# Writing a linear-attention read-out transposed, by 32-column tiles, so that the layer behind it needs no transposes

## Chip, cores, metric

One of the eight cores of a Trainium2 chip. The metric is the device time of one execution in microseconds (us), median of several, without the profiler's own span being used for it.

## The reference, cut to what matters

```python
def _attn_ref(q, k, v, alpha):                      # (4, 8, 768, 48) each
    for t in range(S):
        state = alpha[:, :, t, :, None] * state + einsum('bhd,bhe->bhde', k[:, :, t], v[:, :, t])
        y[:, :, t] = einsum('bhd,bhde->bhe', q[:, :, t], state)

def _moe_ref(x, w_in, w_out, g_ln):                 # x is y as (3072, 384); w_in (384, 1024)
    h = x @ w_in
    solu = h * softmax(h)
    ln = (solu - mean(solu)) / sqrt(var(solu) + 1e-06) * g_ln
    return ln @ w_out
```

The kernel works in 24 tiles of 128 tokens, four batches side by side, six tiles of each in turn. In a tile the recurrence becomes masked scores (128x128 a head), a read of the state carried from the tile before, and an update of the state. The first tile of each batch has no state to read. All matmuls are in fp32, and w_in and w_out arrive as 64-bit numbers and are converted on the chip.

## The kernel before: the parts that matter

```python
ps_tp = pool("ps_tp", 2, space=PS)     # transposes, two buffers for all of them
...
def scores(n):                          # per pair j of heads, the two heads in two row halves
    for j in range(NP):
        for i in range(2):
            nc.tensor.matmul(a[i][:, j], lhsT=d["kT"][heads[i], j], rhs=d["qT"][heads[i], j], ...)
...
def read_out(n):
    y = ps_o.tile([P, H, D], FP, tag="o", name="y")         # tokens on partitions
    if c:
        for j in range(NP):                                  # state: 4 matmuls, 96 columns moving
            nc.tensor.matmul(y[:, 2*j:2*j+2, :], lhsT=d["qT"][:, j], rhs=states[b][:, j]..., ...)
    for h in range(H):                                       # v: 8 matmuls, 48 columns moving
        nc.tensor.matmul(y[:, h, :], lhsT=d["sT"][:, h % 2, h // 2], rhs=d["v"][:, h], ...)
    nc.scalar.copy(out=d["x"], in_=y...)
...
def x_T(n):                                                  # x to features on partitions
    tp = ps_tp.tile([P, KC, P], FP, tag="tp", name="tp_x")
    for a in range(KC):                                      # KC = 3
        nc.tensor.transpose(out=tp[:, a], in_=d["x"][:, a*P:(a+1)*P], identity=ident)
    nc.scalar.copy(out=d["xT"], in_=tp)
...
# one turn of the loop, cut: loads; transposes of alpha, q (n+1); up projection (n-1), first half;
# scores (n); transposes of k (n+1); up projection, second half; keys_back, read_out, next_state (n);
# down projection (n-3); x_T (n).  A scheduler then orders each engine's instructions.
```

Of the kernel before, what the change touches and what calls it, by code (L numbers as in the profile page):

```python
# [9 lines left out]
FP = mybir.dt.float32  # L10
U8 = mybir.dt.uint8
U32 = mybir.dt.uint32
I32 = mybir.dt.int32
AF = mybir.ActivationFunctionType
ALU = mybir.AluOpType
AX = mybir.AxisListType
P = 128
# [15 lines left out]
def fast_path(ctx, tc, q, k, v, alpha, moe_w_in, moe_w_out, moe_g_ln, out):  # L33
# [9 lines left out]
    nc = tc.nc  # L43
    B, H, S, D = q.shape
    NTOK, DM = out.shape
# [3 lines left out]
    NP = H // 2  # L49
    DP = 64  # L50
    KC = DM // P
# [5 lines left out]
    def pool(name, bufs, **kw):  # L57
        return ctx.enter_context(tc.tile_pool(name=name, bufs=bufs, **kw))

    const = pool("const", 1)  # L60
    vp = pool("vp", 4)
    work = pool("work", 2)
    small = pool("small", 4)
    xtp = pool("xtp", UP + 2)
    hid = pool("hid", DOWN - UP + 1)
    rawp = pool("rawp", 4)
    wtmp = pool("wtmp", 2)
    ps_tp = pool("ps_tp", 2, space=PS)
    ps_a = pool("ps_a", 1, space=PS)
    ps_h = pool("ps_h", 2, space=PS)  # L70
    ps_o = pool("ps_o", 2, space=PS)

    ident = const.tile([P, P], FP, name="ident")
    mask = const.tile([P, P], FP, name="mask")
    ones = const.tile([P, P], FP, name="ones")
    w_in = const.tile([P, KC, DFF], FP, name="w_in")
    w_out = const.tile([P, FC, DM + 1], FP, name="w_out")
# [9 lines left out]
    NIN = 4  # L87
    qn = [const.tile([P, H, DP], FP, name=f"qn{i}") for i in range(NIN)]
    kn = [const.tile([P, H, DP], FP, name=f"kn{i}") for i in range(NIN)]
    an = [const.tile([P, H, DP], FP, name=f"an{i}") for i in range(NIN)]  # L90
    SW = P + 1
    aT = [const.tile([P, NP, SW], FP, name=f"aT{i}") for i in range(2)]
    seed = [const.tile([P, NP, SW], FP, name=f"seed{i}") for i in range(2)]
    hT = [const.tile([P, NP * SW + 1], FP, name=f"hT{i}") for i in range(2)]
    unit = const.tile([P, NP, SW], FP, name="unit")
    states = [const.tile([P, NP, 2, D], FP, name=f"state{b}") for b in range(B)]

    st = [dict() for _ in range(N)]
    halves = [slice(0, DP), slice(DP, 2 * DP)]
# [2 lines left out]
    def place(n):  # L102
        c, b = divmod(n, B)
        return b, c

    def load(n):
        b, c = place(n)
        st[n]["v"] = vp.tile([P, H, D], FP, name="vn")
        for src, dst in (
            (alpha, an[n % NIN][:, :, 0:D]),  # L110
            (q, qn[n % NIN][:, :, 0:D]),
            (k, kn[n % NIN][:, :, 0:D]),
            (v, st[n]["v"]),
        ):
            nc.sync.dma_start(out=dst, in_=src[b, :, c * P : (c + 1) * P, :].rearrange("h p d -> p h d"))

# [50 lines left out]
    def decayed(n):  # L167

        b, c = place(n)
        if c == 0:  # L170
            return
        h4 = hT[n % 2][:, 0 : NP * SW].rearrange("p (j s) -> p j s", s=SW)
        s = states[b].rearrange("p j i e -> p j (i e)")
        nc.gpsimd.tensor_tensor(  # L174
            out=s, in0=s, in1=h4[:, :, 1:2].to_broadcast([P, NP, 2 * D]), op=ALU.mult
        )

    def scores(n):
# [19 lines left out]
        nc.scalar.copy(out=d["kg"], in_=tp)  # L198

    def read_out(n):  # L200
        b, c = place(n)
        d = st[n]
        y = ps_o.tile([P, H, D], FP, tag="o", name="y")
        if c:
            for j in range(NP):
                nc.tensor.matmul(  # L206
                    y[:, 2 * j : 2 * j + 2, :], lhsT=d["qT"][:, j],
                    rhs=states[b][:, j].rearrange("p i e -> p (i e)"),
                    start=(j == 0), stop=False, skip_group_check=True,
                )  # L210
        for h in range(H):
            nc.tensor.matmul(  # L212
                y[:, h, :], lhsT=d["sT"][:, h % 2, h // 2], rhs=d["v"][:, h],
                start=(c == 0 and h == 0), stop=(h == H - 1), skip_group_check=True,
            )
        d["x"] = work.tile([P, DM], FP, name="x")
        nc.scalar.copy(out=d["x"], in_=y.rearrange("p h d -> p (h d)"))

    def next_state(n):
        b, c = place(n)  # L220
        d = st[n]
        if c == NCH - 1:
            return
        kv = ps_o.tile([P, NP, 2, D], FP, tag="o", name="kv")
        for j in range(NP):
            nc.tensor.matmul(  # L226
                kv[:, j].rearrange("p i e -> p (i e)"), lhsT=d["kg"][:, j],
                rhs=d["v"][:, 2 * j : 2 * j + 2, :], start=True, stop=True,
            )
        for i in range(2):  # L230
            r = halves[i]
            new = states[b][r, :, i]
            if c == 0:
                nc.vector.tensor_copy(out=new, in_=kv[r, :, i])
            else:
                nc.vector.tensor_tensor(out=new, in0=new, in1=kv[r, :, i], op=ALU.add)

    def x_T(n):
        d = st[n]
        tp = ps_tp.tile([P, KC, P], FP, tag="tp", name="tp_x")  # L240
        for a in range(KC):
            nc.tensor.transpose(out=tp[:, a], in_=d["x"][:, a * P : (a + 1) * P], identity=ident)  # L242
        d["xT"] = xtp.tile([P, KC, P], FP, name="xT")
        nc.scalar.copy(out=d["xT"], in_=tp)  # L244

    HF = FC // 2

# [72 lines left out]
    for i in range(NIN):  # L320
        nc.vector.memset(an[i], 1.0)
        nc.gpsimd.memset(qn[i], 0.0)
        nc.gpsimd.memset(kn[i], 0.0)
    load(0)
    nc.scalar.dma_start(
        out=mask, in_=nc.inline_tensor(np.triu(np.ones((P, P), np.float32)), name="mask_c").ap()
# [15 lines left out]
    float64 = moe_w_in.dtype != FP  # L342
    IN, OUT = 512, DM
    pieces = [(0, a, s) for s in range(0, DFF, IN) for a in range(KC)] + [(1, f, 0) for f in range(FC)]

    def words(i):
        kind, c, s = pieces[i]
        rows = slice(c * P, (c + 1) * P)
        src = moe_w_out[rows, :] if kind else moe_w_in[rows, s : s + IN]
        dst = w_out[:, c, 0:DM] if kind else w_in[:, c, s : s + IN]  # L350
        return src, dst

    def fetch(i):
        src, dst = words(i)
        if not float64:
            nc.sync.dma_start(out=dst, in_=src)
            return None
        raw = rawp.tile([P, dst.shape[1], 2], U32, tag="raw", name="raw")
        nc.sync.dma_start(out=raw.rearrange("p f w -> p (f w)"), in_=src.bitcast(U32))
        return raw  # L360

    raws = {}

    def convert(i):
        kind, c, _ = pieces[i]
        _, dst = words(i)
        if float64:
            raw = raws.pop(i)
            lo, hi = raw[:, :, 0], raw[:, :, 1]
            F = dst.shape[1]  # L370
            low = wtmp.tile([P, F], FP, tag="low", name="low")
            top = wtmp.tile([P, F], U32, tag="top", name="top")
            power = wtmp.tile([P, F], U32, tag="power", name="power")
            nc.scalar.activation(out=low, in_=lo, func=AF.Copy, scale=2.0**-52)
            nc.vector.tensor_scalar(
                out=top, in0=hi, scalar1=3, scalar2=0x3FFFFFF8, op0=ALU.logical_shift_left, op1=ALU.bitwise_and
            )
            nc.vector.scalar_tensor_tensor(  # L378
                out=top, in0=hi, scalar=0xC0000000, in1=top, op0=ALU.bitwise_and, op1=ALU.bitwise_or
            )  # L380
            nc.vector.tensor_scalar(out=power, in0=top, scalar1=0xFF800000, scalar2=None, op0=ALU.bitwise_and)
            nc.gpsimd.tensor_tensor(out=low, in0=low, in1=power.bitcast(FP), op=ALU.mult)  # L382
            eng = nc.vector if i % 2 else nc.gpsimd
            eng.tensor_tensor(out=dst, in0=low, in1=top.bitcast(FP), op=ALU.add)
        if kind:

            nc.scalar.mul(out=dst, in_=dst, mul=g_col[:, c : c + 1])
# [47 lines left out]
    for n in range(N + DOWN):  # L435
        if n + 2 < N:
            load(n + 2)
        if n < DOWN:
            mine = range(nout + n * FC // DOWN, nout + (n + 1) * FC // DOWN)
            for i in mine:  # L440
                raws[i] = fetch(i)
        m, l = n - UP, n - DOWN
        now, rise, fall, after = n < N, 0 <= m < N, l >= 0, n + 1 < N
        if after:
            prep_aq(n + 1)
        if l > 0:
            finish(l - 1)
        if now:
            decayed(n)
        if after:  # L450
            prep_scan(n + 1)
        if rise:
            up(m, 0)
        if after:
            prep_q(n + 1)
        if now:
            scores(n)
        if after:
            prep_k(n + 1)
        if n == 0:  # L460
            for i in range(KC, 2 * KC):
                convert(i)
        if rise:
            up(m, 1)
            partial(m)
        if n < DOWN:
            for i in mine:
                convert(i)
        if n == DOWN:
            centre()  # L470
        if now:
            keys_back(n)
            read_out(n)
            next_state(n)
        if fall:
            down(l)
        if now:
            x_T(n)
        if 2 * DOWN <= n < 2 * DOWN + len(pieces):
            in_range(n - 2 * DOWN)  # L480
    finish(N - 1)
# [472 lines left out]
```

## Time and profile before

| | |
|---|---|
| time, median | 490.15 us (489.24 to 491.8, 3 runs); 489.69 with the runs beside the changed kernel |
| busy, whole span | PE 461.1 us, DVE 264.8, POOL 196.1, ACT 172.7 |
| one tile in the middle | 18.43 us, PE full |
| first down projection done, start of its follower | 94.52 us |

PE is TensorE's matmuls, PEld its weight loads, POOL is GpSimd. Lengths of matmuls overlap, so a price is read from differences of starts. The lines themselves stand in the prediction, where each is used. The last row of the table splits the run into a start and the regular rest; this line of the timeline of the kernel before carries it (columns: start, length, engine, line of the kernel, what, count):

```profile
94.52 0.49 PE L242 MATMUL tp_x<-ident,x 128*128 128x128 f32 x3
```

### The profile page before, as it was taken

What the parts mean: (1) busy time and instruction counts of PE and PEld (TensorE: products, weight loads), DVE (VectorE), ACT (ScalarE), POOL (GpSimd) and SP (SyncE); (2) the same over time, 40 slices, a digit from 0 to 9 for tenths busy, and PEclk for the clock granted to TensorE, in tenths of its full rate; (3) what the DMA queues carried; (4) which work ended last, traced back from release to release, by engine and by line L of the source; (5) the groups of instructions that cost most, each with busy time, mean ns of one, the idle gap of its engine ahead of it and who ended that gap; (6) DMA issues with size and microseconds to landing.
All of it is one profiled execution on the core that took longest, in us unless ns stands there. A gap on an engine that the chain in (4) does not pass through costs nothing.

```text
span 490.0 us, 8081 instructions
## 1 busy us (share of the span) xinstructions
PE 461.1 (94%) x3195; PEld 389.1 (79%) x3195; DVE 264.8 (54%) x522; ACT 172.7 (35%) x344; POOL 196.1 (40%) x208
## 2 busy tenths in 40 slices
PE   2488989999999999999999999999999999999993
PEld 1377978798798798798798798798798798788761
DVE  5897798655365275275275275375374264353231
ACT  3143544588333333333232232232233243333210
POOL 6686476442342342342342342342352352352130
PEclk9998769999999999999999999999999999999998
DMA  8795464687133133133133133033031000000001
GB/s 243 182 230 128 114 130 93 169 254 212 30 68 66 29 69 66 25 71 66 23 71 69 22 70 73 19 71 74 19 70 29 16 17 17 17 1 17 17 16 40
DMA packets 107679, 36.92 MB, mean 75 GB/s; under 512 B 100713, under 2 KB 104049, under 8 KB 107633
## 3 DMA queue, kind: packets, MB, share of 16 engines
q1 hardware_dynamic: 107328, 36.19, 30.6%
q8 instruction: 27, 0.44, 0.4%
q14 instruction: 20, 0.16, 0.1%
q10 hardware_dynamic: 304, 0.14, 0.1%
HBM read 31.59 MB, written 4.72 MB: 74 GB/s over the span
## 4 chain that ended last, share of the span: by engine, by line
PE 87%; DVE 6%; POOL 3%; DMA 2%; issue 1%; ACT 0%; SPq 0%; POOLq 0%; DVEq 0%
PE o L290 26%; PE h L258 24%; PE y L212 8%; PE a L183 7%; PE tp L120 7%; PE kv L226 4%; PE y L206 4%; PE tp_k L196 2%; PE o L285 2%; POOL low L382 2%; PE tp_x L242 2%; DVE top L378 1%; DMA raw<-in_moe_w_in_dram 1%; DVE qF L144 1%; PE mean L415 1%
## 5 line engine op out<-in xcount | busy, mean ns | idle before, releaser
L258 PE MATMUL h<-xT,w_in 128*128 128x128 f32 x1152 | 138.4, 277 | 0.0
L258 PEld LDWEIGHTS h<-xT,w_in 128*128 128x128 f32 x1152 | 134.5, 194 | 0.5
L290 PE MATMUL o<-w_out,u 128*128 128x385 f32 x384 | 130.5, 491 | 0.0
L290 PEld LDWEIGHTS o<-w_out,u 128*128 128x128 f32 x384 | 70.9, 190 | 45.0
L311 POOL TENSOR_TENSOR r<-sums,mhalf 128x1 f32<-128x1 f32 x24 | 13.2, 551 | 141.7 <-DVE sums L307 141.7
L300 DVE COPY sums<-o 128x3 f32<-128x3 f32 x24 | 3.9, 160 | 98.9 <-PE o L290 98.9
L244 ACT COPY xT<-tp_x 128x384 f32<-128x384 f32 x24 | 11.5, 479 | 124.8 <-PE tp_x L242 124.8
L212 PE MATMUL y<-vn,sT 128*128 128x48 f32 x384 | 49.4, 283 | 2.4 <-DVE sT L188 2.4
L212 PEld LDWEIGHTS y<-vn,sT 128*128 128x128 f32 x384 | 48.2, 203 | 3.0 <-DVE sT L188 2.8
L183 PE MATMUL a<-qT,kT 48*128 48x128 f32 x384 | 44.3, 311 | 6.3 <-POOL qT L155 5.2
L264 DVE TENSOR_TENSOR u<-h,e 128x512 f32<-128x512 f32 x48 | 32.8, 684 | 31.4 <-ACT e L263 31.3
L134 DVE TENSOR_TENSOR_SCAN hT<-aT,unit 128x516 f32<-128x516 f32 x24 | 31.1, 1295 | 33.8 <-ACT aT L121 33.7
L265 ACT ACTIVATE u<-u 128x512 f32<-128x512 f32 x48 | 30.3, 630 | 51.9 <-DVE u L264 51.8
L183 PEld LDWEIGHTS a<-qT,kT 48*128 48x128 f32 x384 | 33.6, 200 | 14.3 <-POOL qT L155 5.3
L155 POOL TENSOR_TENSOR qT<-qT,qF 128x512 f32<-128x512 f32 x24 | 29.2, 1216 | 38.7 <-DVE qF L144 38.7
L263 ACT ACTIVATE e<-h 128x512 f32<-128x512 f32 x48 | 28.6, 595 | 44.5 <-PE h L258 44.5
L162 POOL TENSOR_TENSOR kT<-kT,hT 128x508 f32<-128x508 f32 x24 | 30.2, 1258 | 21.2 <-ACT kT L121 21.2
L273 POOL TENSOR_TENSOR part_e<-e 128x512 f32<-128x512 f32 x24 | 30.9, 1287 | 17.8 <-ACT e L263 17.8
L174 POOL TENSOR_TENSOR state<-state,hT 128x384 f32<-128x384 f32 x20 | 16.7, 835 | 46.0 <-DVE hT L134 46.0
L144 DVE TENSOR_TENSOR_SCAN qF<-aT,seed 128x516 f32<-128x516 f32 x24 | 32.3, 1344 | 0.7
L188 DVE TENSOR_TENSOR sT<-a,mask 128x512 f32<-128x512 f32 x48 | 31.0, 678 | 0.0
L273 DVE TENSOR_TENSOR part_u<-u 128x512 f32<-128x512 f32 x24 | 18.4, 765 | 15.6 <-ACT u L265 15.6
(87 smaller groups left out, 588.1 us busy)
## 6 DMA issues: line engine op xcount, KB each, us to landing
raw<-in_moe_w_in_dram SPq DMA_DIRECT2D x12, 512.0 KB, 6.1
raw<-in_moe_w_out_dram SPq DMA_DIRECT2D x16, 384.0 KB, 4.5
vn<-in_v_dram SPq DMA_DIRECT2D x24, 192.0 KB, 2.7
an<-in_alpha_dram SPq DMA_DIRECT2D x24, 192.0 KB, 3.3
qn<-in_q_dram SPq DMA_DIRECT2D x24, 192.0 KB, 3.6
kn<-in_k_dram SPq DMA_DIRECT2D x24, 192.0 KB, 2.8
out_dram<-o_sb SPq DMA_DIRECT2D x24, 192.0 KB, 2.0
ident<-ident_c ACTq DMA_DIRECT2D x1, 64.0 KB, 1.9
```

The costliest lines, as they stand in the source:

```text
L120: nc.tensor.transpose(out=tp[:, j], in_=src[:, 2 * j : 2 * j + 2, :], identity=ident)
L134: nc.vector.tensor_tensor_scan(out=h[:, 0 : NP * SW][:, ::-1], data0=a.rearrange("p j s -> p (j s)")[:, ::-1], data1=unit.rearrange("p j s ...
L144: nc.vector.tensor_tensor_scan(out=d["qF"].rearrange("p j s -> p (j s)"), data0=a.rearrange("p j s -> p (j s)"), data1=s.rearrange("p j s ...
L162: nc.gpsimd.tensor_tensor(out=d["kT"][:, :, 0 : P - 1], in0=d["kT"][:, :, 0 : P - 1], in1=hT[n % 2][:, 0 : NP * SW].rearrange("p (j s) -> ...
L183: nc.tensor.matmul(a[i][:, j], lhsT=d["kT"][heads[i], j], rhs=d["qT"][heads[i], j], start=True, stop=True)
L188: nc.vector.tensor_tensor(out=d["sT"][:, i], in0=a[i], in1=mask[:, None, :].to_broadcast([P, NP, P]), op=ALU.mult)
L212: nc.tensor.matmul(y[:, h, :], lhsT=d["sT"][:, h % 2, h // 2], rhs=d["v"][:, h], start=(c == 0 and h == 0), stop=(h == H - 1), skip_group_ ...
L258: nc.tensor.matmul(h[:, f], lhsT=w_in[:, a, (f0 + f) * P : (f0 + f + 1) * P], rhs=d["xT"][:, a], start=(a == 0), stop=(a == KC - 1),)
L264: nc.vector.tensor_tensor(out=d["u"][:, fs], in0=h, in1=d["e"][:, fs], op=ALU.mult)
L265: nc.scalar.activation(out=d["u2"][:, fs], in_=d["u"][:, fs], func=AF.Square)
L273: eng.tensor_tensor(out=t, in0=d[key][:, 0:HF], in1=d[key][:, HF:FC], op=ALU.add)
L290: nc.tensor.matmul(o[:, 0 : DM + 1], lhsT=d["u"][:, f], rhs=w_out[:, f], start=(f == 0), stop=(f == FC - 1), skip_group_check=True,)
```

## The change

The intent: use v and the state as the stationary operand, so that y comes out with features on partitions, as the up projection wants it. 48 features of a head don't fit a group of 32 partitions; so the first 32 of each head fill two blocks of 128 features, and the remaining 16 of two heads share a group in a third. The rows of w_in are loaded in the same order.

```diff
 def read_out(n):
-    y = ps_o.tile([P, H, D], FP, tag="o", name="y")
+    y = ps_o.tile([P, KC, P], FP, tag="o", name="y")
+    def mm(a, r, lhsT, rhs, stop=False):
+        nc.tensor.matmul(y[32*r:32*r+32, a], lhsT=lhsT, rhs=rhs, start=r not in begun, stop=stop,
+                         skip_group_check=True, tile_position=(0, 32*r))
     if c:
-        ... 4 matmuls, rhs = state
+        for a in range(2):
+            for r in range(NP):
+                h = NP*a + r
+                mm(a, r, states[b][:, h//2, h%2], d["qT"][:, h//2])
+        for r in range(NP):
+            mm(2, r, states[b][:, r, 2], d["qT"][:, r])
-    ... 8 matmuls, rhs = v
+    for a in range(2):
+        for r in range(NP):
+            h = NP*a + r
+            mm(a, r, vt[:, h, 0:E0], d["sT"][:, h%2, h//2])
+    for i in range(2):
+        for r in range(NP):
+            mm(2, r, vt[:, 2*r+i, last[i]], d["sT"][:, i, r], stop=i == 1)
-    nc.scalar.copy(out=d["x"], in_=y...)
+    nc.scalar.copy(out=d["xT"], in_=y)
-def x_T(n): ...
@@ loads
-    (v, st[n]["v"]),
+    (v[:, :, :, 0:E0], vt[:, :, 0:E0]), (v[:, :, :, E0:D], vt[:, :, 48:48+E1]),   # E0, E1 = 32, 16
@@ w_in, per piece of 128 rows and 512 columns
-    one transfer of 128 rows
+    4 transfers of 32 rows, or 8 of 16
@@ next_state: the state is updated in four pieces for two; four memsets of v's buffers at the start
```

More of the change, by code (lines that the diff above doesn't have):

```diff
@@ L60, in fast_path @@
     const = pool("const", 1)
-    vp = pool("vp", 4)
     work = pool("work", 2)
@@ L90, in fast_path @@
     an = [const.tile([P, H, DP], FP, name=f"an{i}") for i in range(NIN)]
+    E0, E1 = 32, 16
+    vn = [const.tile([P, H, 80], FP, name=f"vn{i}") for i in range(NIN)]
+    last = [slice(48, 80), slice(32, 64)]
     SW = P + 1
@@ L95, in fast_path @@
     unit = const.tile([P, NP, SW], FP, name="unit")
-    states = [const.tile([P, NP, 2, D], FP, name=f"state{b}") for b in range(B)]
+    states = [const.tile([P, NP, 3, E0], FP, name=f"state{b}") for b in range(B)]
     st = [dict() for _ in range(N)]
@@ L107, in load @@
         b, c = place(n)
-        st[n]["v"] = vp.tile([P, H, D], FP, name="vn")
+        vt = vn[n % NIN]
         for src, dst in (
@@ L112, in load @@
             (k, kn[n % NIN][:, :, 0:D]),
-            (v, st[n]["v"]),
+            (v[:, :, :, 0:E0], vt[:, :, 0:E0]),
+            (v[:, :, :, E0:D], vt[:, :, 48 : 48 + E1]),
         ):
@@ L174, in decayed @@
         nc.gpsimd.tensor_tensor(
-            out=s, in0=s, in1=h4[:, :, 1:2].to_broadcast([P, NP, 2 * D]), op=ALU.mult
+            out=s, in0=s, in1=h4[:, :, 1:2].to_broadcast([P, NP, 3 * E0]), op=ALU.mult
         )
@@ L202, in read_out @@
         d = st[n]
-        y = ps_o.tile([P, H, D], FP, tag="o", name="y")
-        if c:
-            for j in range(NP):
-                nc.tensor.matmul(
-                    y[:, 2 * j : 2 * j + 2, :], lhsT=d["qT"][:, j],
-                    rhs=states[b][:, j].rearrange("p i e -> p (i e)"),
-                    start=(j == 0), stop=False, skip_group_check=True,
-                )
-        for h in range(H):
-            nc.tensor.matmul(
-                y[:, h, :], lhsT=d["sT"][:, h % 2, h // 2], rhs=d["v"][:, h],
-                start=(c == 0 and h == 0), stop=(h == H - 1), skip_group_check=True,
-            )
-        d["x"] = work.tile([P, DM], FP, name="x")
-        nc.scalar.copy(out=d["x"], in_=y.rearrange("p h d -> p (h d)"))
+        y = ps_o.tile([P, KC, P], FP, tag="o", name="y")
+        begun = set()
+        def mm(a, r, lhsT, rhs, stop=False):
+            nc.tensor.matmul(
+                y[32 * r : 32 * r + 32, a], lhsT=lhsT, rhs=rhs, start=r not in begun, stop=stop,
+                skip_group_check=True, tile_position=(0, 32 * r),
+            )
+            begun.add(r)
+        if c:
+            for a in range(2):
+                for r in range(NP):
+                    h = NP * a + r
+                    mm(a, r, states[b][:, h // 2, h % 2], d["qT"][:, h // 2])
+            for r in range(NP):
+                mm(2, r, states[b][:, r, 2], d["qT"][:, r])
+        vt = vn[n % NIN]
+        for a in range(2):
+            for r in range(NP):
+                h = NP * a + r
+                mm(a, r, vt[:, h, 0:E0], d["sT"][:, h % 2, h // 2])
+        for i in range(2):
+            for r in range(NP):
+                mm(2, r, vt[:, 2 * r + i, last[i]], d["sT"][:, i, r], stop=i == 1)
+        d["xT"] = xtp.tile([P, KC, P], FP, name="xT")
+        nc.scalar.copy(out=d["xT"], in_=y)
     def next_state(n):
@@ L223, in next_state @@
             return
-        kv = ps_o.tile([P, NP, 2, D], FP, tag="o", name="kv")
+        kv = ps_o.tile([P, NP, 2, 64], FP, tag="o", name="kv")
+        vt = vn[n % NIN]
         for j in range(NP):
             nc.tensor.matmul(
-                kv[:, j].rearrange("p i e -> p (i e)"), lhsT=d["kg"][:, j],
-                rhs=d["v"][:, 2 * j : 2 * j + 2, :], start=True, stop=True,
+                kv[:, j], lhsT=d["kg"][:, j], rhs=vt[:, 2 * j : 2 * j + 2, 0:64], start=True, stop=True,
             )
@@ L231, in next_state @@
             r = halves[i]
-            new = states[b][r, :, i]
-            if c == 0:
-                nc.vector.tensor_copy(out=new, in_=kv[r, :, i])
-            else:
-                nc.vector.tensor_tensor(out=new, in0=new, in1=kv[r, :, i], op=ALU.add)
-    def x_T(n):
-        d = st[n]
-        tp = ps_tp.tile([P, KC, P], FP, tag="tp", name="tp_x")
-        for a in range(KC):
-            nc.tensor.transpose(out=tp[:, a], in_=d["x"][:, a * P : (a + 1) * P], identity=ident)
-        d["xT"] = xtp.tile([P, KC, P], FP, name="xT")
-        nc.scalar.copy(out=d["xT"], in_=tp)
+            for new, add in (
+                (states[b][r, :, i], kv[r, :, i, 0:E0]),
+                (states[b][r, :, 2, E1 * i : E1 * i + E1], kv[r, :, i, 48 : 48 + E1]),
+            ):
+                if c == 0:
+                    nc.vector.tensor_copy(out=new, in_=add)
+                else:
+                    nc.vector.tensor_tensor(out=new, in0=new, in1=add, op=ALU.add)
     HF = FC // 2
@@ L323, in fast_path @@
         nc.gpsimd.memset(kn[i], 0.0)
+        nc.gpsimd.memset(vn[i], 0.0)
     load(0)
@@ L347, in words @@
         kind, c, s = pieces[i]
-        rows = slice(c * P, (c + 1) * P)
-        src = moe_w_out[rows, :] if kind else moe_w_in[rows, s : s + IN]
-        dst = w_out[:, c, 0:DM] if kind else w_in[:, c, s : s + IN]
-        return src, dst
-    def fetch(i):
-        src, dst = words(i)
-        if not float64:
-            nc.sync.dma_start(out=dst, in_=src)
-            return None
-        raw = rawp.tile([P, dst.shape[1], 2], U32, tag="raw", name="raw")
-        nc.sync.dma_start(out=raw.rearrange("p f w -> p (f w)"), in_=src.bitcast(U32))
+        if kind:
+            return w_out[:, c, 0:DM], [(slice(0, P), moe_w_out[c * P : (c + 1) * P, :])]
+        heads_rows = moe_w_in[:, s : s + IN].rearrange("(h d) f -> h d f", d=D)
+        if c < 2:
+            parts = [(slice(E0 * r, E0 * r + E0), heads_rows[NP * c + r, 0:E0]) for r in range(NP)]
+        else:
+            parts = [(slice(E1 * h, E1 * h + E1), heads_rows[h, E0:D]) for h in range(H)]
+        return w_in[:, c, s : s + IN], parts
+    def fetch(i):
+        dst, parts = words(i)
+        raw = rawp.tile([P, dst.shape[1], 2], U32, tag="raw", name="raw") if float64 else None
+        for rows, src in parts:
+            if float64:
+                nc.sync.dma_start(out=raw[rows].rearrange("p f w -> p (f w)"), in_=src.bitcast(U32))
+            else:
+                nc.sync.dma_start(out=dst[rows], in_=src)
         return raw
@@ L365, in convert @@
         kind, c, _ = pieces[i]
-        _, dst = words(i)
+        dst, _ = words(i)
         if float64:
@@ L476, in fast_path @@
             down(l)
-        if now:
-            x_T(n)
         if 2 * DOWN <= n < 2 * DOWN + len(pieces):
```

## The prediction

> **What bounds the kernel now.** I read the busy shares first, then the slices, then two equal windows in the steady part, then TensorE's timeline of one tile, because that is where a count of instructions turns into time.
>
> ```profile
> PE 461.1 (94%) x3195; PEld 389.1 (79%) x3195; DVE 264.8 (54%) x522; ACT 172.7 (35%) x344; POOL 196.1 (40%) x208
> ...
> PE   2488989999999999999999999999999999999993
> PEclk9998769999999999999999999999999999999998
> ```
>
> TensorE is busy in every slice from about 25 us to 482 us; the others are half idle. Only the first two slices and the last one are somebody else's. The windows below are two tiles one after the other. The columns after the window are its length, then PE, PEld, DVE, ACT and POOL.
>
> ```profile
> 244.19:262.62 18.43, 18.43 (x138) 15.70 (x137) 9.33 (x19) 5.90 (x12) 6.50 (x7) 1.00 0.26 55
> 262.61:281.04 18.43, 18.43 (x137) 15.70 (x136) 9.33 (x19) 5.90 (x12) 6.49 (x7) 1.00 0.25 54
> ```
>
> A tile repeats every 18.43 us with TensorE full in all of it, DVE half idle and the DMA engines at a quarter. So in the steady part a microsecond off TensorE's stream is a microsecond off the span, 24 times over (20 tiles with a state to read, 4 without). The price of each kind of matmul comes from the starts in the timeline (columns: start, length, engine, line, what, count); the lengths overlap, so I divide differences of starts.
>
> ```profile
> 251.64 1.03 PE L206 MATMUL y<-state,qT 128*128 128x96 f32 x8
> 252.51 1.91 PE L212 MATMUL y<-vn,sT 128*128 128x48 f32 x16
> 254.25 1.10 PE L226 MATMUL kv<-vn,kg 128*128 128x96 f32 x8
> 255.19 0.31 PE L285 MATMUL o<-ones,sum_e 128*128 128x1 f32 x2
> 255.36 0.36 PE L285 MATMUL o<-ones,sum_u 128*128 128x1 f32 x2
> 255.58 5.43 PE L290 MATMUL o<-w_out,u 128*128 128x385 f32 x16
> 260.85 0.49 PE L242 MATMUL tp_x<-ident,x 128*128 128x128 f32 x3
> 261.18 0.60 PE L120 MATMUL tp<-ident,an 128*128 128x128 f32 x4
> 261.71 0.48 PE L183 MATMUL a<-qT,kT 48*128 48x128 f32 x2
> 262.12 0.66 PE L120 MATMUL tp<-ident,qn 128*128 128x128 f32 x4
> 262.61 2.84 PE L258 MATMUL h<-xT,w_in 128*128 128x128 f32 x24
> 265.39 1.16 PE L183 MATMUL a<-qT,kT 48*128 48x128 f32 x14
> 266.47 0.66 PE L120 MATMUL tp<-ident,kn 128*128 128x128 f32 x4
> 266.96 2.84 PE L258 MATMUL h<-xT,w_in 128*128 128x128 f32 x24
> 269.64 0.60 PE L196 MATMUL tp_k<-ident,kT 128*128 128x128 f32 x4
> ```
>
> Each matmul of the program is two records here (8 of y from v make x16). Spacings: h, 128 columns moving, (269.64-266.96)/24 = 112 ns a record. y from v, only 48 moving, (254.25-252.51)/16 = 109 ns. y from state, 96 moving, 0.87/8 = 109 ns. The down projection, 385 moving, 5.27/16 = 329 ns. A short moving side saves nothing below 128: with 128 stationary columns some 110 ns is the floor, and the read-out runs at that floor with 48 columns of 128 in use. That is the waste that the change aims at.
>
> Scores are different: 48 rows, two heads in two halves of the array. Fourteen records (7 matmuls) from 265.39 to 266.47 are 77 ns each, under the floor, so two of them run together. How well, and what it costs to begin and end, the same lines tell: 24 records of h from 262.61 should end at 262.61+24x0.112 = 265.29; the transposes of kn start at 266.47 and take 0.05 us over their 4x0.11. So the block costs 266.47-265.29+0.05 = 1.23 us. Seven matmuls in alternate halves fill 4 slots of 2x112 = 0.223 us, 0.89 us; the other **0.34 us** is the price of one excursion into tiles and back. Check on the lone pair at 261.71: transposes of an should end at 261.62, those of qn start at 262.12 and are 0.05 us long: 0.55 us, and 0.223+0.34 = 0.56.
>
> **What the Trainium skill says.** "TensorE: Matmul & The Clock Gate", Part 2, LDWEIGHTS: the load takes its number of columns over 1.2 per ns, 107 ns for 128; the trace agrees (109 ns floor). The same page, Part 3 on packing small matmuls: outputs at different 32-partition groups of PSUM land in different column groups of the array and run at the same time, starts about 4 ns apart, three such at M=32 giving 2.38x. The trace has only the row form of this (scores), where it agrees; no run shows columns yet. "TensorEngine Tiling (Array Packing)", Key Properties: a change of tiling mode drains TensorE; the 0.34 us agrees. "FP8 and Floating Point Precision", TensorE Precision Notes: true FP32 takes four passes; two records a matmul, each at half the column rate, agree.
>
> **The change part by part, one tile with a state.**
> 1. Removed: read-out as 8+16 records, 254.25-251.64 = 2.61 us.
> 2. Removed: three transposes of x, 261.18-260.85 = 0.33 us, with both copies on ACT (2x0.48 us) made one. ACT is 32% busy in the window; that part is worth nothing by itself.
> 3. Added: 28 matmuls (4 heads x 2 + 4 for the state, 8 + 8 for v) of 32 stationary columns and 128 moving. They go round the four column groups, so 7 rounds. If four run together as two do in scores, a round is 2x112 = 0.223 us, 7 rounds are 1.56 us, and with one excursion of 0.34 it is 1.90 us.
> 4. Moved: the built order of instructions shows something that the diff doesn't. Before, the scores of most tiles stand in two blocks, one or three matmuls and then the rest (52 blocks in all); after, all 8 stand together in each of 24 tiles. Eight matmuls fill the same 4 slots as seven, so the lone block's 0.55 us goes. The 24 new excursions of the read-out are thus paid by 28 old ones of the scores.
> 5. kv gets 128 moving columns for 96: at the 110 ns floor, 0. State update on DVE in four pieces for two, perhaps +0.3 us a tile on an engine that is 51% busy: 0 on the path. decayed keeps its 384 elements.
>
> Sum: 2.61+0.33-1.90+0.55 = 1.59 us a tile, 16.84 for 18.43. Twenty tiles: 31.8 us.
>
> A tile without a state: 16 matmuls, 4 rounds, 0.89+0.34 = 1.23 for 1.74, and 0.33: 0.84 us. Four of those would be 3.4 us, but they lie where conversions of the weights also bind (DVE at 8 or 9 tenths in many early slices); I take 1.5.
>
> Startup, against: four more memsets on GpSimd ahead of unit and states (0.53 us per 512 columns there, so about 0.65 each, 2.6 us); w_in in 32 issues for 6, twice. Six issues took 12.46 us on the queue before, at 243 GB/s, so bytes bound them; 32 at the 0.4 us of the short issues are 13 us: little changes. v in runs of 128 and 64 bytes for 192 adds a quarter to the small packets, with the DMA engines at 26%. TensorE's new order has 14 matmuls of h before the second tile's transposes; it stalls until the fifth piece of w_in is converted, near 30 us, and catches up since h is then done. I charge 3 us.
>
> 490.15-31.8-1.5+3 = **460 us**.
>
> **The rivals.**
> (a) Column tiles do not overlap in fp32. Then 28x0.223+0.34 = 6.58 us for 2.61: with the 0.33 and 0.55 a tile is 3.1 us longer, 62 us in twenty, and 1.8 us in each of the other four: about 560. For it: all four tiles stream all 128 partitions at once, which scores don't (they read different rows). Against: the page's 2.38x.
> (b) Only two at a time, or a limit on records. Scores take 4 records (two loads, two matmuls) in 112 ns, 28 ns each; four tiles need 14 ns each, which no line of the trace shows. At 28 ns, 28x4 records are 3.1 us and the tile is 2.61+0.33+0.55-3.14-0.34 = 0.0 shorter: about 490. Partly so, 475.
> (c) A wait takes the place of the work: masked scores on DVE come late for the shortened stream. Now the last sT ends at 269.64 and the v part starts at 270.95; the part between (h, keys back, state) hardly shrinks, so 1.3 us of slack stay. If they were late by 0.5 us a tile, 470.
> (d) The clock: slices 4 to 6 ran at 0.8, 0.7 and 0.6; another pattern of early stalls could give or take some 5 us.
>
> **Range and chances.** Four tiles together 0.73; halfway or issue-bound 0.14; serial 0.08; something at the start or a new wait eating most of it 0.05. Within the first case the spread is the round (0.223 to 0.25 us: 20x7x0.027 = 4 us), the start (5 us) and the clock (5 us). That gives 451 to 478 for 8 in 10; faster by over 2% 0.82, within 2% 0.09, slower 0.09.
>
> **What would show each step.** The period of a tile in the middle should be 16.8 us, TensorE still full. The read-out should take 1.9 us from its first start to kv's, starts of four records within 30 ns, rounds every 0.223 us; at 3.5 us rival (b) holds, at 6.6 rival (a). Scores should be one block of 16 records costing 1.23 us. tp_x gone. The first down projection, at 89.25 us now, should start within 5 us of that. Idle on TensorE released by DVE's sT, in the middle, would be (c). The prediction fails if column tiles overlap less than row tiles do.

## The result, and the profile after

The changed kernel takes **465.4 us** (463.94 to 467.11, 4 runs) for 489.69: ratio 0.950, 95% interval 0.945 to 0.955. Ratios here are the mean time of one kernel's fast runs over the mean of the other's in the same rounds, so they are not quite the ratio of the medians. The result is correct.

The page of the changed kernel, its busy shares and slices:

```profile
PE 416.6 (90%) x3827; PEld 341.2 (74%) x3827; DVE 278.0 (60%) x562; ACT 161.9 (35%) x320; POOL 198.8 (43%) x212
...
PE   2546848889999999999999999999999999999992
PEclk9996986999999999999999999999999999999997
```

There are 632 more matmul records, and PE is busy 44.5 us less. But PE's digits are low for longer at the beginning. Two tiles in the middle (window, its length, then PE, PEld, DVE, ACT and POOL busy, the clock, the DMA share and GB/s):

```profile
252.07:268.81 16.74, 16.74 (x165) 13.93 (x164) 9.97 (x21) 5.45 (x10) 6.81 (x7) 1.00 0.32 61
268.81:285.55 16.74, 16.74 (x166) 13.93 (x164) 9.96 (x21) 5.44 (x10) 6.80 (x7) 1.00 0.31 60
```

A tile takes 16.74 us for 18.43, with PE still full. The timeline of PE for one of them:

```profile
252.07 0.60 PE L127 MATMUL tp<-ident,an 128*128 128x128 f32 x4
252.51 0.60 PE L127 MATMUL tp<-ident,qn 128*128 128x128 f32 x4
252.94 2.84 PE L274 MATMUL h<-xT,w_in 128*128 128x128 f32 x24
255.72 1.16 PE L190 MATMUL a<-qT,kT 48*128 48x128 f32 x16
256.81 0.66 PE L127 MATMUL tp<-ident,kn 128*128 128x128 f32 x4
257.30 2.84 PE L274 MATMUL h<-xT,w_in 128*128 128x128 f32 x24
259.98 0.60 PE L203 MATMUL tp_k<-ident,kT 128*128 128x128 f32 x4
260.51 0.86 PE L216 MATMUL y<-qT,state 128*32 128x128 f32 x24
261.19 1.06 PE L216 MATMUL y<-sT,vn 128*32 128x128 f32 x32
262.18 1.16 PE L248 MATMUL kv<-vn,kg 128*128 128x128 f32 x8
263.18 0.28 PE L301 MATMUL o<-ones,sum_e 128*128 128x1 f32 x2
```

The 24 records of the state part take 261.19-260.51 = 0.68 us, three rounds of eight at 0.227 us; one record by one at the old floor of 109 ns they would have taken 2.6 us. From the first record to kv the whole read-out, 56 records, takes 262.18-260.51 = 1.67 us, against 2.61 us for 24 records before. The first four records start within 20 ns of one another. The gap before it, 260.51 less 259.98+4x0.109, is 0.09 us: part of the price of the excursion. The scores stand in one block: sixteen records, and by the sum of the prediction (256.81 - (252.94+24x0.112) + 0.05) they cost 1.23 us, what fourteen cost before.

The start went the other way. The follower of the first down projection begins here:

```profile
101.13 0.60 PE L127 MATMUL tp<-ident,an 128*128 128x128 f32 x4
```

From there to the end of the span are 462.2-101.1 = 361.1 us; before they were 490.0-94.5 = 395.5. So the regular part is 34.4 us shorter and the start 6.6 us longer, net 27.8, the difference of the two profiled spans.

These are two single executions: the slowest of the kernel before (491.76 us) and the fastest of the changed one (463.94). The medians differ by 24.3 us. If the regular part gains the same 34.4 in every execution, which was not measured, the start lost some 10 us in a typical execution and not 6.6. How much a start moves by itself shows in b2_scores below: TensorE does the same up to its first down projection as in the kernel before, and yet the follower begins at 92.31 us there, for 94.52 (granted clock up to there 0.94 for 0.89). Read differences of 2 or 3 us in the start with this in mind.

### The profile page after: what moved, and what is told of

It reads as the page before. It is cut to its first block, busy times and chain, and to the rows that moved or that the text cites. A ratio compares the mean times of both kernels' runs of the same rounds, so it can differ in the third digit from the quotient of the medians.

```text
span 462.2 us, 9424 instructions
## 1 busy us (share of the span) xinstructions
PE 416.6 (90%) x3827; PEld 341.2 (74%) x3827; DVE 278.0 (60%) x562; ACT 161.9 (35%) x320; POOL 198.8 (43%) x212
## 4 chain that ended last, share of the span: by engine, by line
PE 80%; DVE 11%; POOL 6%; issue 1%; ACT 1%; DMA 0%; SPq 0%; POOLq 0%; DVEq 0%; ACTq 0%
PE o L306 27%; PE h L274 26%; PE y L216 7%; PE tp L127 7%; PE a L190 5%; PE kv L248 4%; POOL low L406 2%; PE tp_k L203 2%; PE o L301 2%; DVE top L402 2%; DVE qF L151 1%; DVE power L405 1%; DVE top L399 1%; DVE sT L195 1%; DVE hT L141 1%; DVE w_out L408 1%
## 5 line engine op out<-in xcount | busy, mean ns | idle before, releaser
L274 PE MATMUL h<-xT,w_in 128*128 128x128 f32 x1152 | 141.3, 279 | 12.5 <-POOL w_in L408 7.2
L128 ACT COPY aT<-tp 128x512 f32<-128x512 f32 x24 | 14.0, 585 | 129.6 <-PE tp L127 129.6
L216 PE MATMUL y<-sT,vn 128*32 128x128 f32 x768 | 29.2, 285 | 11.1 <-DVE sT L195 11.1
L169 POOL TENSOR_TENSOR kT<-kT,hT 128x508 f32<-128x508 f32 x24 | 28.5, 1189 | 17.3 <-ACT kT L128 17.1
L141 DVE TENSOR_TENSOR_SCAN hT<-aT,unit 128x516 f32<-128x516 f32 x24 | 29.6, 1232 | 8.3 <-ACT aT L128 8.2
L190 PE MATMUL a<-qT,kT 48*128 48x128 f32 x384 | 28.8, 291 | 5.9 <-POOL qT L162 5.6
L216 PEld LDWEIGHTS y<-sT,vn 128*32 128x32 f32 x768 | 22.9, 115 | 13.7 <-DVE sT L195 13.3
L151 DVE TENSOR_TENSOR_SCAN qF<-aT,seed 128x516 f32<-128x516 f32 x24 | 30.2, 1259 | 1.2 <-DVE seed L149 0.5
L190 PEld LDWEIGHTS a<-qT,kT 48*128 48x128 f32 x384 | 24.1, 193 | 8.9 <-POOL qT L162 5.7
L292 POOL TENSOR_TENSOR part_e<-part_e 128x256 f32<-128x256 f32 x24 | 27.7, 1154 | 1.9
```

Of the source, the lines that this page charges most:

```text
L141: nc.vector.tensor_tensor_scan(out=h[:, 0 : NP * SW][:, ::-1], data0=a.rearrange("p j s -> p (j s)")[:, ::-1], data1=unit.rearrange("p j s ...
L151: nc.vector.tensor_tensor_scan(out=d["qF"].rearrange("p j s -> p (j s)"), data0=a.rearrange("p j s -> p (j s)"), data1=s.rearrange("p j s ...
L216: nc.tensor.matmul(y[32 * r : 32 * r + 32, a], lhsT=lhsT, rhs=rhs, start=r not in begun, stop=stop, skip_group_check=True, tile_position=( ...
L274: nc.tensor.matmul(h[:, f], lhsT=w_in[:, a, (f0 + f) * P : (f0 + f + 1) * P], rhs=d["xT"][:, a], start=(a == 0), stop=(a == KC - 1),)
```

## The experiments

Three questions: what the 1.69 us of a tile consist of; whether the order round the four column groups is what makes them run together; and why the start is longer.

### The parts of a tile: before, without the transposes of x (b1_no_xT)

```diff
-        nc.scalar.copy(out=d["x"], in_=y.rearrange("p h d -> p (h d)"))
+        nc.scalar.copy(out=d["xT"].rearrange("p a s -> p (a s)"), in_=y.rearrange("p h d -> p (h d)"))
...
-        if now:
-            x_T(n)
```

> The kernel before without the transposes of x: the copy of y is used as if it were transposed already, so the result is wrong on purpose. Theory: besides 0.33 us of transposes a tile (24 x 0.33 = 7.9 us) the scores fall back into one block, because the transposes of q no longer have to wait for a buffer of the shared transpose pool, and that is worth another 0.55 us in some 20 tiles, 11 us: together 19 us, about 471 us, ratio 0.961, tile period 17.55 us for 18.43. Rival: the split of the scores costs nothing, as the same matmuls run either way; then only 7.9 us go, 482 us, ratio 0.984.

Measured: 475.28 us, ratio 0.971 (0.967 to 0.975). Its output is wrong, which doesn't matter for the time. The window of one tile:

```profile
253.36:270.92 17.56, 17.56 (x134) 15.12 (x133) 9.27 (x19) 5.44 (x10) 6.74 (x7) 1.00 0.26 57
```

The period is what the theory said, 17.56 us, and the scores do stand in one block. Taking out three transposes a tile thus gave 0.87 us, over twice their 0.33. The total fell short of the 471 us expected because the expectation counted 24 tiles: the start did not gain (the follower of the first down projection begins at 94.11 us here), so only the regular 20 count, 17.4 us at most.

### The scores alone in one block (b2_scores)

```diff
+            if rise and n >= 5:
+                with tc.issue_after(behind[0].ins):     # last matmul of the first half of the up projection
+                    scores(n)
```

> The kernel before, with nothing changed but that from the sixth tile on the scores are queued behind the first half of the up projection, which makes them one block of 8 (18 tiles). Theory of 0.34 us an excursion and pairs of 0.22 us: 18 x 0.55 = 10 us less, 480 us, ratio 0.980. Rival: the split is free: 490 us, ratio 1.00.

Measured: 481.77 us, ratio 0.984 (0.981 to 0.987), correct. Nothing is left out here, the same instructions run, and still 8 us are gone: an excursion into tiles has a price (of the old 0.55 us, 0.22 are the lone matmul's own slot, which fits into the one block). The period is 18.01 us, 0.42 less where 0.55 was expected. The timeline shows where the rest is:

```profile
255.02 0.60 PE L120 MATMUL tp<-ident,an 128*128 128x128 f32 x4
255.46 0.36 PE L206 MATMUL y<-state,qT 128*128 128x96 f32 x2
255.76 0.66 PE L120 MATMUL tp<-ident,qn 128*128 128x128 f32 x4
256.25 2.84 PE L259 MATMUL h<-xT,w_in 128*128 128x128 f32 x24
```

The scheduler put two records of the state part into the place, 0.22 us that have to run anyway; the transposes of q begin at 255.76, not at 255.68, and take 0.49 us for 0.44. These 0.13 us are a wait. The transposes of x, alpha and q follow one another and share two buffers, so q's need the copy of x out of one. That copy on ScalarE, first in the kernel before, then here:

```profile
261.38 0.48 ACT L244 COPY xT<-tp_x 128x384 f32<-128x384 f32 x1 [6.39 <-PE tp_x L242]
255.22 0.48 ACT L244 COPY xT<-tp_x 128x384 f32<-128x384 f32 x1 [6.39 <-PE tp_x L242]
```

Before, it ends at 261.86 and q's transposes begin at 262.12: there the lone pair of scores holds them up, and the wait is hidden behind it. Here it ends at 255.70 and they begin at 255.76: now the copy holds them up. So the lone block cost its 0.55 us, as the prediction had it, but taking it out uncovers 0.13 us of wait, and 0.42 is left as gain. With the transposes of x gone, the wait goes too (b1, next to its 0.33).

So the 1.69 us of a tile divide as: scores in one block 0.42 (18.43 to 18.01), transposes of x with that wait 0.45 (to 17.56), the read-out by columns 0.82 (to 16.74). Half of the gain is not the new matmuls' own. The last part is what is left over, and holds what kv and the sums gained (below).

### Two column groups at a time, then one (a2_two, a1_one)

The same 28 matmuls in another order.

```diff
-        if c:
-            for a in range(2):
-                for r in range(NP): ...          # all four groups in turn
+        for g in ((0, 1), (2, 3)):               # a1_one: ((0,), (1,), (2,), (3,))
+            if c:
+                for a in range(2):
+                    for r in g: ...
+            ... the same for the v part
```

> The changed kernel with the same 28 matmuls of the read-out in another order: first all of column groups 0 and 1 in turn, then all of 2 and 3. Theory: matmuls run together only where neighbours in the order lie in different column groups, so two at a time: 14 slots of 0.219 us for 7, 1.53 us more in 20 tiles and 0.88 us in 4, 34 us: about 499 us, ratio 1.02. Rival: the engine picks independent work from further ahead, or the limit is elsewhere: 465 us, ratio 0.95.

> The changed kernel with the read-out of one column group after the other, 7 matmuls each. a2_two showed that two at a time take 2.78 us for 1.66, some 12 slots of 0.219 us instead of 14, as the next group's first matmuls were already taken beside the last of the group before. Theory: overlap is with the next few matmuls of the order only: 28 slots less about 3 at each of three borders, 19 to 28 slots, 4.2 to 6.2 us a read-out, 520 to 565 us. Rival: a look-ahead that is longer than that: below 500 us.

Measured: a2_two 486.73 us, ratio 0.992 (0.990 to 0.995); a1_one 531.86 us in one look. Both correct. The order alone is worth 21 and 66 us, so it is what makes the groups run together; this speaks against the rival. But a2_two is 12 us better than expected. Its timeline (x2 and the like count records, two a matmul):

```profile
253.95 0.85 PE L216 MATMUL y<-qT,state 128*32 128x128 f32 x12
254.63 0.71 PE L216 MATMUL y<-sT,vn 128*32 128x128 f32 x10
255.08 0.30 PE L216 MATMUL y<-qT,state 128*32 128x128 f32 x2
255.18 0.28 PE L216 MATMUL y<-sT,vn 128*32 128x128 f32 x2
...
255.76 1.04 PE L216 MATMUL y<-sT,vn 128*32 128x128 f32 x16
256.73 1.16 PE L249 MATMUL kv<-vn,kg 128*128 128x128 f32 x8
```

The first pair's matmuls are 12 records of the state and then 16 of v, in that order in the program, and also in the order that the scheduler built for TensorE. Yet after ten of the sixteen the second pair's state records begin, at 255.08, while six of the first pair's are still to come. TensorE takes work for free column groups from a little further on, and four run together around the border. The read-out takes 256.73-253.95 = 2.78 us, 12 slots of 0.219 plus the gap after the last, not 14. In a1_one it takes 5.01 us, some 22 slots for 28: two gained at each of three borders.

```profile
291.29 0.84 PE L216 MATMUL y<-qT,state 128*32 128x128 f32 x6
...
296.30 1.16 PE L249 MATMUL kv<-vn,kg 128*128 128x128 f32 x8
```

So the look-ahead is real but short, one or two matmuls of a group; the rotation is needed. (Periods: 17.85 us in a2_two; 1.11 x 20 = 22 us over 465.4 give 487.6, and 486.7 was measured.)

### The price of an excursion into column tiles (d1_split)

In c4_order (below), the four transposes of the scaled keys are moved between the two parts of the read-out.

```diff
+        if c:
+            with tc.issue_after(last_mm[0].ins):   # last matmul of the state part
+                back = keys_back(n)
+            with tc.issue_after(back.ins):
+                v_part()
```

> c4_order with the read-out cut in two on purpose: in the 20 tiles with a state, the four transposes of the scaled keys stand between its state part (12 matmuls) and its v part (16). The same instructions run, only a second excursion into column tiles is paid. Theory, 0.34 us an excursion for column tiles as for the row tiles of scores: tile period 17.08 us for 16.74, 6.8 us in all, 466 us, ratio 0.950. Rival: column tiles switch for less or nothing: 459 us, ratio 0.937. If the copy of the keys then comes late for kv, the trace shows a wait of kv and the difference is larger.

Measured: 464.53 us, ratio 0.948 (0.945 to 0.951), correct; c4_order had 458.91. Window and timeline:

```profile
235.81:252.83 17.02, 17.02 (x166) 13.89 (x165) 9.56 (x21) 5.37 (x10) 6.53 (x7) 1.00 0.31 59
```

```profile
243.81 0.86 PE L221 MATMUL y<-qT,state 128*32 128x128 f32 x24
244.60 0.66 PE L206 MATMUL tp_k<-ident,kT 128*128 128x128 f32 x4
245.19 1.08 PE L221 MATMUL y<-sT,vn 128*32 128x128 f32 x32
246.20 1.16 PE L263 MATMUL kv<-vn,kg 128*128 128x128 f32 x8
```

The period grows from 16.74 to 17.02 us: a second excursion costs 0.28 us, and 20 x 0.28 = 5.6 us is the measured difference. The copy of the keys did not come late: kv waits for it once in the regular part, 0.4 us. The 0.34 us that the scores gave is the right size, somewhat high.

### The start: a transfer for each piece, joined (c3_joined) or plain (c2_six)

```diff
-            parts = [(slice(E0*r, E0*r+E0), heads_rows[NP*c+r, 0:E0]) for r in range(NP)]
+            parts = [(slice(0, P), heads_rows[NP*c : NP*c+NP, 0:E0])]       # c3_joined: right rows, one transfer
+            parts = [(slice(0, P), moe_w_in[c*P:(c+1)*P, s:s+IN])]          # c2_six: rows not reordered
```

> The changed kernel with each piece of w_in brought by one transfer instead of 4 or 8, rows still reordered, result right. Theory: the many issues of w_in are what made the start 6 us later (first down projection done at 101.1 us for 94.5 us), by delaying the loads of the second tile and by turning the order of the instructions round; with six issues the order of the start is like that of before, and the time falls by 6 us to about 459 us, ratio 0.938. Rival: the start is longer because of the memsets of v, v in two transfers and the four state copies; then it stays at 465 us, ratio 0.950.

> The changed kernel with w_in brought by six plain transfers of 128 rows each, rows not reordered, so the result is wrong on purpose; the instructions stand in the same order as in c3_joined. Theory: c3_joined was slow because its six transfers, whose rows jump every 32 or 16, moved some 116 GB/s for 240 and held up the small loads behind them (the second tile's alpha was waited for 19.6 us); plain ones do not: about 459 us, ratio 0.938. Rival: the order of the instructions of c3_joined is what is slow: about 490 us, ratio 1.0.

Measured: c3_joined **497.93 us**, ratio 1.019 (1.013 to 1.026), correct, and far from both theories. c2_six 463.94 us, ratio 0.950 (0.945 to 0.954). Its output is wrong, which doesn't matter for the time. PE's waits in the first 100 us (total, times, longest), first of c3_joined, then of c2_six:

```profile
PE tp L127 <- DMA an<-in_alpha_dram: 29.9, 2, 19.6
```

```profile
PE tp L127 <- DMA an<-in_alpha_dram: 10.4, 2, 6.0
```

And the windows in which those weights arrive, c3_joined and c2_six (the last three numbers: clock, DMA share, GB/s):

```profile
10.00:40.00 30.00, 5.43 (x25) 4.39 (x25) 9.16 (x18) 3.78 (x7) 6.06 (x5) 0.61 0.50 125
```

```profile
5.00:25.00 20.00, 7.68 (x39) 6.14 (x40) 14.89 (x22) 5.35 (x9) 13.05 (x17) 0.70 0.92 216
```

Both kernels have the same built order of instructions on every engine and the same bytes; only the shape of six transfers differs. Joined, they keep half of the DMA engines' time busy and move 125 GB/s, and alpha of the second tile, queued behind them, is late. The Trainium skill says so, and I had not looked there: "DMA: Bandwidth & Descriptors", Rules for kernel authors, "Use all 16 engines": an outermost dimension of fewer than 16 confines a transfer to that many engines. It is 4 or 8 here. The trace agrees with the halved share; how many engines worked, it doesn't show.

The other half of c3_joined's theory falls with c2_six. Six plain transfers do not give the 6 us back, 463.9 us for 465.4. That alone doesn't clear the number of issues, as c2_six also has another order of instructions than the changed kernel; c4_order, next, keeps all 32 issues and settles it.

### The start: the order of the instructions (c4_order, c6_load1)

What stood in the start of the changed kernel? DVE's waits in the first 102 us, and its timeline:

```profile
DVE u L280 <- ACT e L279: 6.0, 1, 6.0
```

```profile
22.77 1.63 DVE L402 SCALAR_TENSOR_TENSOR top<-raw,top 128x512 uint32<-128x512 uint32 x1
30.43 0.69 DVE L280 TENSOR_TENSOR u<-h,e 128x512 f32<-128x512 f32 x1 [6.02 <-ACT e L279]
31.04 0.42 DVE L405 TENSOR_SCALAR power<-top 128x512 uint32<-128x512 uint32 x1
32.90 0.69 DVE L408 TENSOR_TENSOR w_in<-low,top 128x512 f32<-128x512 f32 x1 [1.45 <-POOL low L406]
```

DVE took nothing past u in these 6.0 us. The scheduler put u of the first tile between the two halves of a conversion of w_in; u needs e, e needs h, and h, begun at 21.07 us, had to wait for its third piece of w_in until 25.58, so that e began only at 29.80. Meanwhile three pieces of w_in waited behind u, and TensorE, at h, had the second tile's transposes behind it (they begin at 38.92 us for 20.82 before). The fix gives two orders, one on each engine (the scheduler then arranged the other engines' work anew by itself):

```diff
+        if n == UP:     # first up projection: on DVE behind the last conversion of w_in, on PE behind tile 1's transposes
+            with tc.issue_after(marks["dve"]), tc.issue_after(marks["pe"]):
+                up(m, 0)
```

> The changed kernel with one thing fixed in the order of the start: the first up projection is queued on TensorE behind the second tile's transposes and on DVE behind the last conversion of w_in. Theory: what made the start 6 us longer is a wait in a circle: DVE stood 6.0 us at u of the first tile (for e, for h, for w_in's third piece) with three conversions behind it, and TensorE stood at h with the second tile's transposes behind it. With the order fixed the first down projection is done some 6 us sooner, about 459 us, ratio 0.938. Rival: DVE simply has more work in the start (four state copies, longer conversions), the waits only moved: 465 us, ratio 0.950.

Measured: **458.91 us** (458.45 to 459.9), ratio 0.937 (0.934 to 0.939), correct. It is the best of all versions run. DVE's wait at u is gone, and TensorE no longer waits for w_in (7.2 and 3.9 us in the changed kernel). Which of the two orders did more was not tried. The follower of the first down projection begins 1.0 us after that of the kernel before:

```profile
95.53 0.60 PE L128 MATMUL tp<-ident,an 128*128 128x128 f32 x4
```

The period in the middle is 16.74 us as in the changed kernel; so the 6 us come from the start, as said.

c6_load1 moves the loads of the second tile forward as well:

```diff
-    for i in range(2 * KC): raws[i] = fetch(i)
-    load(1)
+    for i in range(KC): raws[i] = fetch(i)
+    load(1)
+    for i in range(KC, 2 * KC): raws[i] = fetch(i)
```

> As c4_order, and the loads of the second tile are issued between the two halves of w_in rather than behind all its 32 issues. Theory: the second tile's inputs land at about 15 us for 24 us, its preparation fills the time in which conversions are waited for: 2 to 3 us less than c4_order, about 456 us, ratio 0.932. Rival: conversions on DVE and GpSimd bind the start whatever is loaded first: as c4_order.

Measured: 464.48 us, ratio 0.948 (0.946 to 0.950), correct. My theory fell, and the rival that it would be like c4_order as well: it is 5.6 us worse. TensorE's waits in its first 100 us:

```profile
PE h L277 <- POOL w_in L411: 5.7, 2, 4.2
PE mean L444 <- ACT w_out L416: 5.2, 2, 5.0
```

The second tile's preparation now stands before the later conversions on DVE; TensorE waits for w_in, which it doesn't in c4_order, and later 5.2 us for w_out, where in c4_order it waits 0.5. That what the early loads gave was lost to the conversions behind them fits these waits; no run isolates it.

### v by one transfer (d2_vone)

```diff
-            (v[:, :, :, 0:E0], vt[:, :, 0:E0]), (v[:, :, :, E0:D], vt[:, :, 48 : 48 + E1]),
+            (v, vt[:, :, 0:D]),
```

> c4_order with v brought by one transfer of 192-byte runs as in the kernel before, in place of two of 128 and 64 bytes; columns 48 to 63 then hold zeros, so the result is wrong on purpose. Theory: with the DMA engines under a third busy in the middle and TensorE waiting for no DMA there, the smaller packets cost nothing in the middle and at most 1 us in the start: 458 to 459 us, ratio 0.936. Rival: they hold up the loads of the start, where TensorE waits 8.9 us for alpha in all: 455 us, ratio 0.93.

Measured: 461.19 us, ratio 0.943 (0.939 to 0.947). Its output is wrong, which doesn't matter for the time. Taking away the small packets of v gained nothing, and TensorE waits for alpha 8.9 us in all as in c4_order, so the rival falls. That it is 2.3 us slower than c4_order, with fewer packets and the same order on TensorE, was not expected; its follower of the first down projection begins 1.0 us later, at 96.57 us. The scheduler gave DVE, ScalarE and GpSimd another order here; whether that is the cause stays open, and so a cost of the packets under some 2 us is not excluded. It warns that 2 us in this start should not be read as an effect.

## Why the prediction was right, point by point

- **The time.** 460 us with 451 to 478 was predicted, 465.4 measured; it is 5 us too low, as two terms of the sum were off in opposite directions: the regular part gained more than predicted, and the start lost more. That they partly cancel is luck.
- **Bound.** Right: PE is full in the middle before and after, and no wait of PE in the middle is found after. Rival (c), scores late on DVE, came only in the start (DVE's mask is waited for 11.1 us there in all, 2.4 before). Rival (d), the clock: up to the follower of the first down projection the profiles show 0.90 granted for 0.89 before, and 1.00 in the middle of both, so it doesn't explain the difference of these two.
- **Read-out by columns.** Right in mechanism and size: four records start together and a round takes 0.219 to 0.227 us for 0.223. From the end of tp_k (259.98+4x0.109) to kv's proper begin (263.18-8x0.112) are 1.87 us, and 1.90 were predicted. Rivals (a) and (b) are out; a1_one and a2_two show what they would have looked like. (That the old floor of 109 ns is the load of 128 stationary columns, as the prediction has it, no run separates: in a1_one 32 columns are loaded and 128 move, and records still start 109 ns apart.)
- **Transposes of x, scores in one block.** Predicted 0.33+0.55 = 0.88, measured 0.87 (b1_no_xT). Right in the sum. The division was slightly off: the lone block alone gave 0.42, as a wait of 0.13 behind it came to light, and this went only with the transposes.
- **kv and the rest.** Taken as 0; kv takes 8x0.112 = 0.89 for 0.94 us (by the spacing of its records; the first one's wait is counted with the excursion) and the two sums 0.36 for 0.39. With these, a tile gained 1.69 us for 1.59.
- **Regular part.** Predicted 31.8 us less, measured 34.4.
- **The start.** This term was mis-sized. "It stalls until the fifth piece of w_in is converted, near 30 us, and catches up since h is then done": the fifth piece let TensorE go on at 38.34 us and not near 30, and it did not catch up. 3 us were charged, less 1.5 gained, so 1.5 in all; 6.6 us longer was measured in the two profiles, some 10 if the medians are taken (34.4 less 24.3). The first down projection began at 95.19 us, 5.9 after the old one, outside the 5 us that I allowed. The stall was seen in the built order beforehand; what was missed is that DVE would wait for the same h, with three conversions behind it (6.0 us). c4_order takes the wait away, and the start is 1.0 us longer than before in the profiles, some 3 us by the medians (34.4 less 31.1). Memsets, transfers and state pieces together cost something of that size; they were not tried one by one.
- **Transfers.** Right, as far as the runs tell: 32 issues for 6 change little (c2_six, 1.5 us, within its range; c4_order keeps the 32), and so do v's small packets (d2_vone, but for its open 2 us).

## What to carry to other kernels

When TensorE is the bound, count its changes of tiling as work (0.28 to 0.34 us each here) and look at the built order: removing an instruction from a shared buffer's queue can give more than the instruction took. Put matmuls of different column groups next to one another in the program; a small look-ahead exists, and it doesn't save a bad order (486.7 and 531.9 us for 465.4 here). After a change, compare the start apart from the regular part: a scheduler may turn it round, and two fixed orders were worth 6 us of 465 here.

## What the Trainium skill lacked or had wrong

- "TensorE: Matmul & The Clock Gate", Part 3, "What overlaps and what doesn't": it says that matmuls start in strict program order. In a2_two records of the second pair of column groups start at 255.08 us, six records of the first pair, earlier in the program and in the built order, after them.
- The same page gives 2.38x for three column tiles and no case of fp32. Here, in fp32, four run fully together: 8 records a round of 0.219 to 0.227 us, where one after the other they take 8x0.109.
- "TensorEngine Tiling (Array Packing)", Key Properties: a change of mode drains, without a price. Runs here: 0.34 us for an excursion into row tiles and back (by the sums on the kernel before, with which b2_scores agrees), 0.28 us for column tiles (d1_split).
